# One ring of buffers for every loaded weight, float64 pieces converted in place, and other assumptions for loads in the list schedule

## The chip, the cores and the metric

The kernel runs on one core of one Trainium2 chip. The metric is the device time of one execution in microseconds, the median of several runs. The engines are TensorE (PE: products, and PEld: its weight loads), VectorE (DVE), ScalarE (ACT), GpSimd (POOL) and SyncE (SP, which here only issues transfers). Each works through its own list of instructions in order.

## The reference

Three layers follow one another on 1152 tokens of width 512: attention in a window of 64 positions, a layer of 8 experts where each token goes to one (with a capacity), and a dense layer:

```
h = x @ w_in                       # w_in  [512, 2048] float64
relu6 = np.clip(h + 3.0, 0.0, 6.0)
g = h * relu6 / 6.0
return (g @ w_out).astype(np.float32)   # w_out [2048, 512] float64
```

The expert layer computes `max(x @ w1[e], 0) @ w2[e]` with w1 [8, 512, 1024] and w2 [8, 1024, 512] in float32, times the gate's probability. [...]

## The kernel before, in words

**Products.** Every factor is kept as two float32r parts, high and low, and each product is three passes (high by high, low by high, high by low; `PASSES` and `mm`, L247-249). `split_ops` makes the two parts of a weight piece: ScalarE rounds it to the high part (L263), VectorE subtracts that for the low part (L268). Both go to a tile `wt`, of which there are eight halves.

**Units.** The work is cut into units of 256 columns of a hidden layer. 32 units (e0 to e31) belong to the experts, four to an expert, each with two halves of 512 KB that `weights_in` loads on the SP queue (L276 for w1, L279 for w2). Eight (d0 to d7) belong to the dense layer. A dense unit has four pieces of 512 KB of float64: pieces 0 and 1 from w_in for the up product, 2 and 3 from w_out for the down product. Eight expert units are tiny (64 tokens): TensorE multiplies their loaded float32 weights directly (L1468 up, L1493 down), so their buffers are held until the product has read them.

**Conversion.** A float64 piece arrives as 1024 words per partition, where low and high words alternate, so words of one kind lie 8 bytes apart. `conv64` turns it into 512 float32 values in six steps: ScalarE takes the absolute value of the high words (L207) and rounds them in place (L210); VectorE clamps (L214), shifts (L218), joins with the high words (L223) and adds the low words (L232, `t_add`).

**Buffers before.** Expert halves and the finished dense pieces share the ring `raw` of six buffers (4 KB per partition); float64 pieces have a ring of their own, `raw64`, of three. For d0 and d1 (`NSC = 2`) POOL's queue loads the pieces (L198, L201) during the expert stage, the converted pieces go from tiles `t64` to DRAM on the same queue (L235), and later come back as halves of `raw` (L1130). The pieces of d2 to d7 are loaded by SP and converted straight into halves of `raw`.

**The order of the work.** A list scheduler in Python writes the instructions. Products of TensorE and the steps that depend on them are written in a fixed order. Loads, conversions and splits are jobs with a due unit; `fill(limit)` (behind each product) emits the earliest due jobs whose estimated start fits before the limit, plus `SLACK` for engines or `SLACK_D` for loads, and `need` forces what a product is about to read. A load is assumed to have landed 2 us after its issue. A job's place in an engine's list is fixed once written; at run time an instruction waits for semaphores, and all behind it on that engine wait too.

**The dense layer.** It runs in four groups of tokens. The first takes tokens 0 to 639 through units d0 to d3, two steps of 128 columns for each: an up product (48 products of 320 tokens by three passes for two steps), then relu6 on ScalarE (L1554), its product with h on VectorE (`gf`, L1557), the split of that into `g` (L1560, L1563), and the down product of 15. The two parts of x come from L1384 on ScalarE and L1386 on VectorE.

Of the kernel before, what the change touches and what calls it, by code (L numbers as in the profile page):

```python
# [23 lines left out]
def tile_kernel(ctx, tc, q, k, v, w_gate, w1, w2, w_in, w_out, out, cap):  # L24
# [153 lines left out]
    NSC = 2  # L178
    cv = ctx.enter_context(tc.tile_pool(name="cv", bufs=2))
    wd_dram = [dram.tile([128, UW], F32, name=f"wd_dram{u}") for u in range(NSC)]  # L180
# [5 lines left out]
    def conv64(u, i, dst):  # L186

        box = {}  # L190

        queue = nc.gpsimd if u < NSC else nc.sync

        def load():
            box["raw"] = raw = cv.tile([128, 2 * HW], U32, name="raw64", bufs=NR64)
            if i < 2:
                src = w_in32[256 * i : 256 * i + 256, 2 * FU * u : 2 * FU * u + 2 * FU]
                queue.dma_start(raw.rearrange("p (c f) -> p c f", c=2), src.rearrange("(c p) f -> p c f", p=128))  # L198
            else:
                r0 = FU * u + 128 * (i - 2)  # L200
                queue.dma_start(raw, w_out32[r0 : r0 + 128, :])  # L201
            w = raw.rearrange("p (n t) -> p n t", t=2)
            box["lo"], box["hi"] = w[:, :, 0], w[:, :, 1]

        def c_abs():
            box["c"] = cv.tile([128, HW], U32, name="c64", bufs=NC64)
            nc.scalar.activation(box["c"].bitcast(F32), box["hi"].bitcast(F32), AF.Abs)  # L207
# [29 lines left out]
        return load, c_abs, c_round, c_clamp, c_shift, a_join, t_add, store  # L237

    NR64, NC64, NT64 = 3, 2, 2
# [83 lines left out]
    with ExitStack() as actx:  # L323
# [482 lines left out]
        def early_gather(e):  # L806
            box["xE"] = t = cv.tile([128, HW], U32, name="c64", bufs=NC64).bitcast(F32)
# [30 lines left out]
        def early_relu(u):  # L838
            def run(e):
                if "hfE" not in box:  # L840
                    box["hfE"] = cv.tile([128, HW], F32, name="t64", bufs=NT64)
                    box["hE"] = cv.tile([128, HW], F32, name="t64", bufs=NT64)
# [29 lines left out]
        def early_out(e):  # L872
            box["yE"] = t = cv.tile([128, HW], U32, name="c64", bufs=NC64).bitcast(F32)
# [87 lines left out]
        def first_gather(e):  # L961
            box["x0"] = t = cv.tile([128, HW], U32, name="c64", bufs=NC64).bitcast(F32)
# [59 lines left out]
    NRAW = 3  # L1022
# [8 lines left out]
    rawp = ctx.enter_context(tc.tile_pool(name="rawp", bufs=2 * NRAW))  # L1031
# [36 lines left out]
    SLACK, SLACK_D = 0.5, 4.0  # L1068
    BIAS = {"V": 0.6, "A": 0.1}
    AHEAD = (3.0, 1.5)  # L1070
    ZDUE = 3
# [25 lines left out]
    r_raw, r_wt, r_64, r_ct, r_t = Ring(2 * NRAW), Ring(2 * NWT), Ring(NR64), Ring(NC64), Ring(NT64)  # L1097
# [6 lines left out]
    wt_at, raw_at = {}, {}  # L1104
    for m in range(len(units)):
        for h in range(2):
            raw_at[m, h] = len(raw_at)
            if not whole(m):
                wt_at[m, h] = len(wt_at)
    raw_t, raw_ready, wt, half_ready, stored, pieces = {}, {}, {}, {}, {}, {}  # L1110
# [7 lines left out]
    def load_job(m, h):  # L1118
        kind, s, u = units[m]

        def gate():
            if kind == "d" and stored.get((u, h), 0) < 2:
                return None
            return r_raw.free(raw_at[m, h])

        def run(e, fin):
            take_raw(m, h)
            t = raw_t[m, h]
            if kind == "d":
                nc.gpsimd.dma_start(t, wd_dram[u][:, HALF * h : HALF * h + HALF])  # L1130
            else:
                if u == 0:
                    e_of[s] = expert(s)
                x = e_of[s]
                weights_in(t, x, u, h)
            raw_ready[m, 2 * h] = raw_ready[m, 2 * h + 1] = fin + 2.0
            if whole(m):
                half_ready[m, h] = fin + 2.0
# [4 lines left out]
    def conv_job(u, i, m=None):  # L1143
        h = i // 2
        ix = {}

        def dst():
            return None if m is None else raw_t[m, h][:, HW * (i % 2) : HW * (i % 2) + HW]

        load, c_abs, c_round, *mid, t_add, store = conv64(u, i, dst)  # L1150

        def gate_load():
            a = 0.0 if m is None or (m, h) in raw_t else r_raw.free(raw_at[m, h])
            b = r_64.free()
            return None if a is None or b is None else max(a - 2.0, b)

        def run_load(e, fin):
            if m is not None and (m, h) not in raw_t:
                take_raw(m, h)
            ix["raw"] = r_64.take()  # L1160
            load()
            return (fin if m is not None else spend("D", 1.46, fin)) + 2.0
# [13 lines left out]
        def run_add(e, fin):  # L1176
            if m is None:
                ix["t"] = r_t.take()
            t_add()
            r_64.rel[ix["raw"]] = r_ct.rel[ix["ct"]] = fin  # L1180
            if m is not None:
                raw_ready[m, i] = fin + 0.2
            return fin + 0.2

        def run_store(e, fin):
            store()
            r_t.rel[ix["t"]] = fin + 5.0
            stored[u, h] = stored.get((u, h), 0) + 1
            return fin

        now = lambda: 0.0
        ops = [({"D": 1.46} if m is not None else {"P": 1.1}, gate_load, run_load), ({"A": 0.6}, r_ct.free, run_abs)]
        ops.append(({"A": 0.57}, now, plain(c_round)))
        ops += [({"V": c}, now, plain(fn)) for c, fn in zip((0.34, 0.34, 0.61), mid)]
        ops.append(({"V": 0.61}, now if m is not None else r_t.free, run_add))
        return ops + ([({"P": 1.1}, now, run_store)] if m is None else [])
# [791 lines left out]
```

## Time and profile before

| | |
|---|---|
| median of 3 runs | 435.39 us (435.08 to 438.6) |
| profiled execution | 434.86 us, of which the span of the trace is 432.9 |
| PE busy | 406.1 us, 94% |
| DVE busy | 290.0 us, 67% |
| ACT busy | 241.4 us, 56% |
| DMA moved | 73.89 MB, 171 GB/s on average |
| granted clock of TensorE | 0.992 over the span |

Busy shares are means over stages that differ. The attention ends near 65 us, the expert stage runs to about 222, the first group of the dense layer from there to 277, and the other groups to the end. In the trace w_in and w_out of the dense layer are called `in_moe_w_in_dram` and `in_moe_w_out_dram`, the expert weights `in_moe_w_dram`, and both `raw` and `raw64` are called `raw`.

### The profile page before, as it was taken

How to read it: one execution, taken by the hardware profiler on the slowest of the kernel's cores; microseconds unless marked ns; L12 is line 12 of the kernel's file. 1: busy time of each engine (PE TensorE's matmuls, PEld its weight loads, DVE VectorE, ACT ScalarE, POOL GpSimd, SP SyncE). 2: the span in 40 equal slices, each digit the busy share in tenths (PEclk: the TensorE clock that was granted, in tenths of full speed). 3: DMA queues.
4: the chain of work that ended last, by engine and by line, in shares of the span. 5: the costliest groups of instructions: out<-in, count | busy, mean ns of one | idle time of the engine just before them, and what ended most of it. 6: DMA issues, size and time to landing. Idle time of an engine off the chain costs nothing.

```text
span 432.9 us, 8533 instructions
## 1 busy us (share of the span) xinstructions
PE 406.1 (94%) x3055; PEld 345.4 (80%) x3055; DVE 290.0 (67%) x800; ACT 241.4 (56%) x527; POOL 62.5 (14%) x128
## 2 busy tenths in 40 slices
PE   7999888798899999999999999999999999999991
PEld 4887664597778989987899898888888888899981
DVE  2888967687789999717579999989843222323430
ACT  4886773584569887526587766577543222322320
POOL 8633405025022001000200000000000000200210
PEclk9999999999999999999999999999999999999996
DMA  9997857989999999656924465543100000100101
GB/s 172 203 232 179 273 216 233 363 288 372 364 313 372 287 344 286 198 180 216 385 91 135 117 172 162 150 142 105 44 0 0 2 0 2 60 37 2 49 30 51
DMA packets 67762, 73.89 MB, mean 171 GB/s; under 512 B 31008, under 2 KB 49440, under 8 KB 67712
## 3 DMA queue, kind: packets, MB, share of 16 engines
q1 hardware_dynamic: 63760, 59.79, 46.6%
q0 software_dynamic: 3952, 13.47, 8.4%
q8 instruction: 26, 0.43, 0.4%
q14 instruction: 24, 0.20, 0.1%
HBM read 66.44 MB, written 6.82 MB: 169 GB/s over the span
## 4 chain that ended last, share of the span: by engine, by line
PE 65%; DVE 14%; DMA 10%; ACT 5%; issue 3%; POOL 0%; POOLq 0%; ACTq 0%; DVEq 0%; SPq 0%
PE banks L249 52%; DVE wt L268 4%; DMA raw<-in_moe_w_dram 4%; PE banks L506 2%; DMA c<-x_dram,eI 2%; PE banks L624 2%; DMA c<-x_dram,sidx 1%; PE banks L1493 1%; PE banks L1468 1%; PE banks L570 1%; PE banks L606 1%; DVE c L223 1%; DVE g L1563 1%; PE banks L663 1%; ACT wt L263 1%
## 5 line engine op out<-in xcount | busy, mean ns | idle before, releaser
L249 PE MATMUL banks<-x,wt 128*128 128x320 f32 (+3 forms) x576 | 107.4, 337 | 1.8 <-DVE wt L268 1.4
L249 PEld LDWEIGHTS banks<-x,wt 128*128 128x128 f32 x576 | 94.3, 188 | 12.2 <-DVE wt L268 2.2
L268 DVE TENSOR_TENSOR wt<-raw,wt 128x512 fp32r<-128x512 f32 x128 | 82.8, 684 | 14.9 <-ACT wt L263 14.3
L249 PE MATMUL banks<-wt,g 128*128 128x512 f32 x384 | 92.8, 390 | 0.0
L263 ACT CAST wt<-raw 128x512 fp32r<-128x512 f32 x128 | 74.6, 620 | 15.8 <-DMA raw<-in_moe_w_dram 9.4
L249 PEld LDWEIGHTS banks<-wt,g 128*128 128x128 f32 x384 | 71.6, 188 | 14.2
L1557 DVE SCALAR_TENSOR_TENSOR gf<-r,banks 128x320 f32<-128x320 f32 (+3 forms) x48 | 26.5, 552 | 54.5 <-ACT r L1554 54.3
L1554 ACT ACTIVATE r<-banks,c_three 128x320 f32<-128x320 f32 (+3 forms) x48 | 27.8, 579 | 58.3 <-PE banks L249 58.1
L249 PE MATMUL banks<-xT,wt 128*128 128x256 f32 (+2 forms) x288 | 39.0, 284 | 0.5 <-DVE wt L268 0.3
L249 PEld LDWEIGHTS banks<-xT,wt 128*128 128x128 f32 x288 | 35.1, 191 | 2.7 <-DVE wt L268 0.8
L249 PE MATMUL banks<-h,wt 128*128 128x256 f32 (+2 forms) x288 | 37.0, 279 | 0.0
L249 PEld LDWEIGHTS banks<-h,wt 128*128 128x128 f32 x288 | 34.6, 191 | 0.5 <-issue 0.5
L1563 DVE TENSOR_TENSOR g<-gf,g 128x320 fp32r<-128x320 f32 (+2 forms) x40 | 23.4, 584 | 12.3 <-ACT g L1560 11.6
L207 ACT ACTIVATE c<-raw 128x512 f32<-128x512 f32 x32 | 21.7, 677 | 17.1 <-DVE raw L232 6.3
L1560 ACT CAST g<-gf 128x320 fp32r<-128x320 f32 (+2 forms) x40 | 21.3, 533 | 16.3 <-DVE gf L1557 16.2
L1600 POOL DMA_INDIRECT out_dram<-raw,cidx x4 | 4.0, 992 | 163.8 <-ACT raw L1597 156.2
L249 PE MATMUL banks<-wt,xT 128*128 128x256 f32 x144 | 22.1, 294 | 3.0 <-DVE wt L268 2.2
L249 PEld LDWEIGHTS banks<-wt,xT 128*128 128x128 f32 x144 | 18.7, 190 | 5.7 <-DVE wt L268 3.6
L596 ACT ACTIVATE pe<-neg,nmx 128x128 f32<-128x128 f32 x72 | 22.3, 392 | 0.1
L583 DVE CUSTOM_DVE_ANT_0 neg<-banks,tmask 128x128 f32<-128x128 f32 x72 | 16.2, 285 | 9.1 <-PE banks L570 9.1
L223 DVE SCALAR_TENSOR_TENSOR c<-raw,c 128x512 uint32<-128x512 uint32 x32 | 22.0, 686 | 0.4
L210 ACT ACTIVATE raw<-raw 128x512 uint32<-128x512 uint32 x32 | 21.6, 674 | 0.0
(287 smaller groups left out, 556.0 us busy)
## 6 DMA issues: line engine op xcount, KB each, us to landing
raw<-in_moe_w_dram SPq DMA_DIRECT2D x64, 512.0 KB, 6.0
raw<-in_moe_w_in_dram SPq DMA_DIRECT2D x12, 512.0 KB, 3.8
raw<-in_moe_w_out_dram SPq DMA_DIRECT2D x12, 512.0 KB, 3.7
early<-in_moe_w_dram SPq DMA_DIRECT2D x8, 512.0 KB, 7.3
x_dram<-xt SPq DMA_DIRECT2D x9, 256.0 KB, 2.9
q_sb<-in_q_dram SPq DMA_DIRECT2D x8, 256.0 KB, 4.8
k_sb<-in_k_dram SPq DMA_DIRECT2D x8, 256.0 KB, 4.8
v_sb<-in_v_dram SPq DMA_DIRECT2D x8, 256.0 KB, 4.7
```

The lines of the kernel that those rows point to most:

```text
L207: nc.scalar.activation(box["c"].bitcast(F32), box["hi"].bitcast(F32), AF.Abs)
L210: nc.scalar.activation(box["lo"], box["lo"], AF.Copy, scale=2.0 ** -29)
L223: nc.vector.scalar_tensor_tensor(out=box["c"], in0=box["hi"], scalar=0xC0000000, in1=box["c"], op0=ALU.bitwise_and, op1=ALU.bitwise_or,)
L249: nc.tensor.matmul(out, l, r, start=(start and n == 0), stop=(stop and n == len(pairs) - 1))
L263: nc.scalar.copy(hi, r)
L268: V.tensor_tensor(out=lo, in0=r, in1=hi.bitcast(F32), op=ALU.subtract)
L583: V.tensor_tensor_reduce(out=neg[:, hp, :], in0=box["sp", g][:, hp, :], in1=tmask[:, first, :], scale=-1.0, scalar=3.0e38, op0=ALU.add, op ...
L596: nc.scalar.activation(pe[:, hp, :], neg[:, hp, :], AF.Exp, bias=nmx[:, hp : hp + 1], scale=-1.0)
L1554: nc.scalar.activation(r, ph, AF.Relu, bias=c_three)
L1557: V.scalar_tensor_tensor(out=gf, in0=r, scalar=6.0, in1=ph, op0=ALU.min, op1=ALU.mult)
L1560: nc.scalar.copy(hi, gf)
L1563: V.tensor_tensor(out=lo, in0=gf, in1=hi.bitcast(F32), op=ALU.subtract)
```

## The change

There is one ring of eight `raw` buffers for all loads: expert halves and float64 pieces alike, all on the SP queue. It takes as much memory as the two rings, `t64` and the extra tiles did. `t_add` writes its 512 results over the low words of the piece itself, 8 bytes apart, and the splits read them there. d0's four pieces are converted when units 5, 9, 14 and 20 are due (`FIRST_AT`), into four contiguous tiles `first_w`, which stay until the dense layer begins. d1 is converted like d2 to d7, 1.5 units before its use. The stores to DRAM and the reloads are gone. The scheduler takes a load to have landed 3.5 us after its issue, and may write a load 40 us ahead of the limit rather than 4. The order of TensorE's products is the same. The buffers of the early expert (`hfE`, `hE`) are now `first_w[0]` and `first_w[1]`.

```diff
-    def conv64(u, i, dst):
+    def conv64(u, i, dst=None):
         box = {}
-        queue = nc.gpsimd if u < NSC else nc.sync
         def load():
-            box["raw"] = raw = cv.tile([128, 2 * HW], U32, name="raw64", bufs=NR64)
+            box["raw"] = raw = rawp.tile([128, 2 * HW], F32, name="raw").bitcast(U32)
             if i < 2:
                 ...
         def t_add():
-            d = dst()
-            if d is None:
-                box["t"] = d = cv.tile([128, HW], F32, name="t64", bufs=NT64)
-            nc.vector.tensor_tensor(out=d.bitcast(U32), in0=box["c"], in1=box["lo"], op=ALU.add)
-
-        def store():
-            nc.gpsimd.dma_start(wd_dram[u][:, HW * i : HW * i + HW], box["t"])
+            out = box["lo"] if dst is None else dst.bitcast(U32)
+            nc.vector.tensor_tensor(out=out, in0=box["c"], in1=box["lo"], op=ALU.add)
+        return box, (load, c_abs, c_round, c_clamp, c_shift, a_join, t_add)
-    NR64, NC64, NT64 = 3, 2, 2
+    NC64 = 2
+    first_w = [cv.tile([128, HW], F32, name=f"first_w{i}", bufs=1) for i in range(4)]
...
-    NRAW = 3
+    NRAW = 8
+    FIRST_AT = (5, 9, 14, 20)
-    rawp = ctx.enter_context(tc.tile_pool(name="rawp", bufs=2 * NRAW))
+    rawp = ctx.enter_context(tc.tile_pool(name="rawp", bufs=NRAW))
-    SLACK, SLACK_D = 0.5, 4.0
+    SLACK, SLACK_D = 0.5, 40.0
...
+    dense0 = unit_of["d", 0, 0]
     for m in range(len(units)):
+        if m != dense0:
+            for n in range(2 if units[m][0] == "e" else NPC):
+                raw_at[m, n] = len(raw_at)
+            for i in range(NPC):
+                if FIRST_AT[i] == m:
+                    raw_at[dense0, i] = len(raw_at)
...
         def run(e, fin):
             take_raw(m, h)
-            t = raw_t[m, h]
-            if kind == "d":
-                nc.gpsimd.dma_start(t, wd_dram[u][:, HALF * h : HALF * h + HALF])
-            else:
-                ...
-            raw_ready[m, 2 * h] = raw_ready[m, 2 * h + 1] = fin + 2.0
+            ...
+            raw_ready[m, 2 * h] = raw_ready[m, 2 * h + 1] = fin + 3.5
...
         def run_low(e, fin):
             ...
+            if units[m][0] == "d" and m != dense0:
+                r_raw.rel[raw_at[m, i]] = fin
...
-            if kind == "d" and u >= NSC:
-                add_job(m - AHEAD[1] + 0.1 * i, m, conv_job(u, i, m))
+            if m == dense0:
+                add_job(FIRST_AT[i] + 1, FIRST_AT[i], conv_job(m, i))
             elif kind == "d":
-                add_job(m + ZDUE + 0.1 * i, m, conv_job(u, i))
-        if kind == "e" or u < NSC:
+                add_job(m - AHEAD[1] + 0.1 * i, m, conv_job(m, i))
+        if kind == "e":
```

**POOL's list in the expert stage, before.** L801 gathers token rows; L198 and L201 load float64 pieces, L235 stores converted ones.

```order
L801 DMA xg<-x_dram,sidx 64x512
L198 DMA raw_1552<-in_moe_w_in_dram 128x2x512
L198 DMA raw_1554<-in_moe_w_in_dram 128x2x512
L201 DMA raw_1568<-in_moe_w_out_dram 128x1024
L235 DMA wd_dram_101<-t_1666 128x512
L201 DMA raw_1708<-in_moe_w_out_dram 128x1024
L801 DMA xg<-x_dram,sidx 128x512
L235 DMA wd_dram_101<-t_1781 128x512
L198 DMA raw_1826<-in_moe_w_in_dram 128x2x512
L801 DMA xg<-x_dram,sidx 128x512
L235 DMA wd_dram_101<-t_1807 128x512
```

The same place after the change, where gathers are L791:

```order
L1852 CAST eofI_1448<-eofF 128x8
L791 DMA xg<-x_dram,sidx 128x512 x2
L791 DMA xg<-x_dram,sidx 64x512
L791 DMA xg<-x_dram,sidx 128x512 x2
L791 DMA xg<-x_dram,sidx 96x512
L791 DMA xg<-x_dram,sidx 128x512 x2
L791 DMA xg<-x_dram,sidx 80x512
```

Only the gathers are left; the eight loads went to SP's list, the stores and the reloads have no successor.

**VectorE's list at the start of the dense layer, before.** It begins with the two low parts of x. L214, L218, L223 and L232 here convert d2; `gf` and `g` belong to the first up products; wt_3483 is the up half of d1 (third up product).

```order
L1386 TENSOR_TENSOR x2_1616<-banks_82,x2_1616 128x2x208
L214 TENSOR_SCALAR c64_3533<-c64_3533 128x512
L218 TENSOR_SCALAR c64_3533<-c64_3533 128x512
L1557 SCALAR_TENSOR_TENSOR gf_3537<-r6_3536,banks_82 128x320
L223 SCALAR_TENSOR_TENSOR c64_3533<-raw64_3410,c64_3533 128x512
L214 TENSOR_SCALAR c64_3542<-c64_3542 128x512
L1563 TENSOR_TENSOR g_3520<-gf_3537,g_3520 128x320
L1557 SCALAR_TENSOR_TENSOR gf_3562<-r6_3561,banks_82 128x320
L218 TENSOR_SCALAR c64_3542<-c64_3542 128x512
L232 ISA raw_3409<-raw64_3410,c64_3533 128x1024
L1563 TENSOR_TENSOR g_3520<-gf_3562,g_3520 128x320
```

The same place after, with L1363 for L1386, L208, L212, L217 and L224 for the conversion, L258 for the split, L1534 for `gf`. wt_3358 is the up half of d0; raw_3299 and raw_3301 are the last two pieces of d1.

```order
L1363 TENSOR_TENSOR x2_1614<-banks_82,x2_1614 128x2x208
L258 TENSOR_TENSOR wt_3358<-first_w1_102,wt_3358 128x512
L212 TENSOR_SCALAR c64_3413<-c64_3413 128x512
L217 SCALAR_TENSOR_TENSOR c64_3413<-raw_3299,c64_3413 128x512
L224 ISA raw_3299<-raw_3299,c64_3413 128x512x2
L208 TENSOR_SCALAR c64_3472<-c64_3472 128x512
L212 TENSOR_SCALAR c64_3472<-c64_3472 128x512
L217 SCALAR_TENSOR_TENSOR c64_3472<-raw_3301,c64_3472 128x512
L1534 SCALAR_TENSOR_TENSOR gf_3502<-r6_3501,banks_82 128x320
L208 TENSOR_SCALAR c64_3499<-c64_3499 128x512
L224 ISA raw_3301<-raw_3301,c64_3472 128x512x2
```

Two instructions of a conversion stood between x and the first `gf`; now a split of d0 and six of d1's conversion do. Before, all four splits of d0 stood ahead of x; now three of them follow it, the two of its down half between the `gf` further on, and the splits of d1's up half (wt_3509) come after those.

## Rows read from the trace of the kernel before

**Rows 1.** The page's part 1, busy time and share of the span.

```profile
PE 406.1 (94%) x3055; PEld 345.4 (80%) x3055; DVE 290.0 (67%) x800; ACT 241.4 (56%) x527; POOL 62.5 (14%) x128
```

**Rows 2.** Table by stretches: length, busy us of each engine, clock, DMA share, GB/s.

```profile
85.00:130.00 45.00, 41.45 (x335) 35.79 (x334) 35.99 (x91) 28.35 (x62) 11.61 (x16) 1.00 0.99 335
...
180.00:222.20 42.20, 41.56 (x355) 35.61 (x353) 21.69 (x48) 21.43 (x51) 2.19 (x4) 1.00 0.69 235
222.20:277.30 55.10, 53.33 (x299) 48.01 (x299) 51.60 (x106) 38.34 (x75) 0.00 (x0) 1.00 0.46 133
```

**Rows 3.** Waits of TensorE, 85 to 280 us: total us, times, longest.

```profile
PE banks L249 <- DVE wt L268: 3.8, 5, 1.2
PE banks L1468 <- DMA raw<-in_moe_w_dram: 1.1, 1, 1.1
PE banks L249 <- ACT wt L263: 0.6, 1, 0.6
```

**Rows 4.** DMA from 70 to 130 us: sum, software queue, issues with us to landing.

```profile
DMA packets 11812, 20.16 MB, mean 336 GB/s; under 512 B 728, under 2 KB 6892, under 8 KB 11806
...
q0 software_dynamic: 2144, 7.41, 34.2%
...
raw<-in_moe_w_dram SPq DMA_DIRECT2D x25, 512.0 KB, 8.2
raw<-in_moe_w_in_dram POOLq DMA_DIRECT2D x4, 512.0 KB, 8.7
raw<-in_moe_w_out_dram POOLq DMA_DIRECT2D x4, 512.0 KB, 7.3
wd_dram<-t POOLq DMA_DIRECT2D x7, 256.0 KB, 6.2
```

**Rows 5.** Chain of waits that ended last: start us, length, what.

```profile
100.60 12.88 DMA raw<-in_moe_w_dram
```

**Rows 6.** Waits of the SP queue, 60 to 130 us.

```profile
SPq L276 <- PE banks L1468: 11.3, 3, 9.7
```

**Rows 7.** TensorE's timeline: start us, length, shape, [wait before, releaser].

```profile
110.76 2.19 PE L249 MATMUL banks<-xT,wt 128*128 128x256 f32 x12
...
118.20 1.60 PE L249 MATMUL banks<-xT,wt 128*128 128x256 f32 x12
...
199.07 1.94 PE L249 MATMUL banks<-wt,xT 128*128 128x256 f32 x12
...
223.14 7.01 PE L249 MATMUL banks<-x,wt 128*128 128x320 f32 x46 [0.36 <-ACT x L1384]
...
233.42 3.68 PE L249 MATMUL banks<-x,wt 128*128 128x320 f32 x24
...
248.90 3.51 PE L249 MATMUL banks<-x,wt 128*128 128x320 f32 x20 [0.86 <-DVE wt L268]
...
264.15 2.90 PE L249 MATMUL banks<-x,wt 128*128 128x320 f32 x18 [0.50 <-DVE wt L268]
```

**Rows 8.** VectorE's timeline at the dense layer's start.

```profile
223.69 0.43 DVE L214 TENSOR_SCALAR c<-c 128x512 f32<-128x512 f32 x1
224.15 0.43 DVE L218 TENSOR_SCALAR c<-c 128x512 uint32<-128x512 uint32 x1
225.47 0.49 DVE L1557 SCALAR_TENSOR_TENSOR gf<-r,banks 128x320 f32<-128x320 f32 x1 [0.90 <-ACT r L1554]
...
232.70 1.28 DVE L268 TENSOR_TENSOR wt<-raw,wt 128x512 fp32r<-128x512 f32 x2
233.90 0.68 DVE L223 SCALAR_TENSOR_TENSOR c<-raw,c 128x512 uint32<-128x512 uint32 x1
234.62 0.69 DVE L232 CUSTOM_DVE_ANT_0 raw<-raw,c 128x1024 uint16<-128x1024 uint16 x1
```

**Rows 9.** The page's part 5, costliest groups: busy us, mean ns of one.

```profile
L223 DVE SCALAR_TENSOR_TENSOR c<-raw,c 128x512 uint32<-128x512 uint32 x32 | 22.0, 686 | 0.4
L210 ACT ACTIVATE raw<-raw 128x512 uint32<-128x512 uint32 x32 | 21.6, 674 | 0.0
```

More of the change, by code (lines that the diff above doesn't have):

```diff
@@ L177, in tile_kernel @@
     HW = UW // 4
-    NSC = 2
     cv = ctx.enter_context(tc.tile_pool(name="cv", bufs=2))
-    wd_dram = [dram.tile([128, UW], F32, name=f"wd_dram{u}") for u in range(NSC)]
     w_in32 = w_in.bitcast(U32)
@@ L840, in run @@
                 if "hfE" not in box:
-                    box["hfE"] = cv.tile([128, HW], F32, name="t64", bufs=NT64)
-                    box["hE"] = cv.tile([128, HW], F32, name="t64", bufs=NT64)
+                    box["hfE"] = first_w[0]
+                    box["hE"] = first_w[1]
                 if e == "A":
@@ L1118, in load_job @@
     def load_job(m, h):
-        kind, s, u = units[m]
+        _, s, u = units[m]
         def gate():
-            if kind == "d" and stored.get((u, h), 0) < 2:
-                return None
             return r_raw.free(raw_at[m, h])
@@ L1127, in run, with conv_job @@
             take_raw(m, h)
-            t = raw_t[m, h]
-            if kind == "d":
-                nc.gpsimd.dma_start(t, wd_dram[u][:, HALF * h : HALF * h + HALF])
-            else:
[L1132 to L1135, printed above, removed]
-            raw_ready[m, 2 * h] = raw_ready[m, 2 * h + 1] = fin + 2.0
+            if u == 0:
+                e_of[s] = expert(s)
+            weights_in(raw_t[m, h], e_of[s], u, h)
+            raw_ready[m, 2 * h] = raw_ready[m, 2 * h + 1] = fin + 3.5
             if whole(m):
-                half_ready[m, h] = fin + 2.0
+                half_ready[m, h] = fin + 3.5
             return fin
         return [({"D": 1.46}, gate, run)]
-    def conv_job(u, i, m=None):
-        h = i // 2
+    def conv_job(m, i):
+        u = units[m][2]
         ix = {}
[L1147 to L1155, printed above, removed]
+        first = m == dense0
+        b, (load, c_abs, c_round, *mid, t_add) = conv64(u, i, first_w[i] if first else None)
         def run_load(e, fin):
-            if m is not None and (m, h) not in raw_t:
-                take_raw(m, h)
-            ix["raw"] = r_64.take()
+            r_raw.take()
             load()
-            return (fin if m is not None else spend("D", 1.46, fin)) + 2.0
+            raw_t[m, i] = first_w[i] if first else b["lo"].bitcast(F32)
+            return fin + 3.5
         def run_abs(e, fin):
@@ L1176, in run_add @@
         def run_add(e, fin):
[L1177 to L1178 removed]
             t_add()
[L1180 to L1182 removed]
+            r_ct.rel[ix["ct"]] = fin
+            if first:
+                r_raw.rel[raw_at[m, i]] = fin
+            raw_ready[m, i] = fin + 0.2
             return fin + 0.2
[L1185 to L1189, printed above, removed]
         now = lambda: 0.0
[L1192 removed]
+        ops = [({"D": 1.46}, lambda: r_raw.free(raw_at[m, i]), run_load), ({"A": 0.6}, r_ct.free, run_abs)]
         ops.append(({"A": 0.57}, now, plain(c_round)))
         ops += [({"V": c}, now, plain(fn)) for c, fn in zip((0.34, 0.34, 0.61), mid)]
[L1195 to L1196 removed]
+        ops.append(({"V": 0.61}, now, run_add))
+        return ops
     def split_job(m, i):
@@ L1211, in run_high @@
             n = HALF // 2
-            r = raw_t[m, h][:, n * (i % 2) : n * (i % 2) + n]
+            r = raw_t[m, h][:, n * (i % 2) : n * (i % 2) + n] if units[m][0] == "e" else raw_t[m, i]
             high, box["low"] = split_ops(wt[m, h], r, i % 2)
@@ L1675, in dense_again @@
                 for i in range(NPC):
-                    r = wk.tile([128, HW], F32, name="xg", bufs=3)
-                    if u < NSC:
-                        nc.sync.dma_start(r, wd_dram[u][:, HW * i : HW * i + HW])
-                    else:
-                        load, *mid, t_add, _ = conv64(u, i, lambda: r)
-                        for fn in (load, *mid, t_add):
-                            fn()
+                    b, ops = conv64(u, i)
+                    for fn in ops:
+                        fn()
+                    r = b["lo"].bitcast(F32)
                     high, low = split_ops(halves[i // 2], r, i % 2)
@@ L1872, in tile_kernel @@
     est["D"] = max(est["D"], done["rk"] + 1.7)
-    for ring, t in ((r_64, est["P"]), (r_ct, done["g0"] + 4.0), (r_t, done["g0"] + 4.0)):
+    for ring, t in ((r_ct, done["g0"] + 4.0),):
         ring.rel = [t] * ring.n
```

24 lines of the change are left out of this document (12 added, 12 removed).

## The prediction, made before the changed kernel ran

> **What bounds the kernel now.** I read the page's busy times first: TensorE is busy for 406.1 of 432.9 us [rows 1], so at most 27 us of waits can be won, and adding work to another engine costs only where TensorE then waits for it. The table by stretches came next [rows 2]. The stretch from 85 to 130 us has the DMA engines at a share of 0.99 with TensorE 3.55 us short of full; from 180 to 222 VectorE is half idle (21.69 of 42.20 us); from 222 to 277, the first group of the dense layer, VectorE is busy for 51.60 of 55.10 us and TensorE lacks 1.77. So two stretches have little room, one in DMA and one in VectorE, and between them lies one with room in both. Third, the waits of TensorE from 85 to 280 us [rows 3]: 3.8 us for the split weights `wt` of VectorE (five waits), 1.1 for a load, 0.6 for `wt` of ScalarE. Two of the five VectorE waits, 0.86 and 0.50, stand in the dense group [rows 7], which leaves 3.8 - 1.36 = 2.44 in the expert stage.
>
> Who makes them late? The DMA view of 70 to 130 us [rows 4] has 20.16 MB at 336 GB/s; 7.41 MB of it are on the software queue, where the conversion of d0 and d1 lives: eight loads of 512 KB (4 + 4) and seven stores of 256 KB. A load of expert weights takes 8.2 us to land there. In the chain of waits one load holds 12.88 us from 100.60 [rows 5], with the late splits right behind it. And the SP queue itself stood for 9.7 us on the first product of a tiny expert (L1468), whose buffer the next load in line needed [rows 6]: with six buffers, no load could pass it.
>
> **The change part by part.**
>
> *Expert stage.* Removed: eight loads on POOL, eight stores, four reloads (POOL's rows in the order go from stores and loads between the gathers to gathers alone). Added: eight loads on SP, four of them spread at units 5, 9, 14 and 20, of which two fall before unit 10. Of the traffic between 70 and 130 us, 8 x 0.5 + 7 x 0.25 = 5.8 MB go and about 1 MB comes back, 4.8 MB or 14 us at 336 GB/s [rows 4]. The ring grows from six to eight, and by the order of the loads and the count of buffers 15 loads rather than 10 can be issued ahead of the first tiny product. VectorE loses d1's conversions here (four pieces of four instructions), which stand in the same stretch. All three point at the same waits: 2.44 + 1.1 + 0.6 = 4.1 us, plus two products that ran stretched without a recorded wait, 2.19 and 1.94 where the same shape takes 1.60 [rows 7], 0.6 + 0.35. That is 5.0 us in all. Bounds: 0 if the waits only change their cause; the 5.0 plus nothing, since the shorter waits here are for h, which the change doesn't touch. I take -5.0: the load that the chain names now has 14 us of traffic less ahead of it, over its 12.88 us.
>
> *The dense start.* The conversion of d1 moves to just before its use, beside d2's. d0 is already converted, but three of its four splits, and d1's last two conversions, now stand on VectorE behind the second low part of x (the order's rows on VectorE). VectorE runs in order, so I price the list. Two independent splits start 0.60 us apart (1.28 for two, of 0.68 each); 16 instructions from 225.47 to 232.70 take 7.23 us, four of them of the wide kind, so the others cost (7.23 - 2.4) / 12 = 0.40; a wide instruction that needs the result of the one before starts after 0.72 (233.90 to 234.62) rather than 0.60, a narrow one after 0.46 (223.69 to 224.15) [rows 8].
> (a) The first product's second low part of `wt` starts at 223.69 at the earliest, when that slot held an L214 before [rows 8], and is ready 0.69 later, at 224.4. TensorE resumed at 223.14 and comes to it four products (0.15 each, 7.01 for 46) on [rows 7], 223.7: +0.7.
> (b) From 223.69 to the second low part of the third up product there are 27 instructions, 12 wide: 12 x 0.60 + 15 x 0.40 + 0.3 for dependent neighbours = 13.5, so ready at 237.2, and its first low part at 236.6. Before, up product three began at 233.42 [rows 7]; it asks for the first low part four products later, 234.0, and with (a) 234.7. The wait is 1.9, and 0.3 more for the second: 2.2.
> (c) To the fifth up product's second low part 30 more, 13 wide: 7.8 + 6.8 + 0.5 = 15.1, ready at 252.3 and 251.7. TensorE asks at 248.04 (248.90 less its wait of 0.86 [rows 7]) plus 2.9, 250.9: 0.8 + 0.3 = 1.1.
> Behind it the list has fewer instructions per step than TensorE has time for, and the 0.50 of the seventh product goes. Together 0.7 + 2.2 + 1.1 = 4.0 after against 0.86 + 0.50 = 1.36 before: **+2.6**. Bounds: +0.5 if d1's pieces get their VectorE time during 180 to 222 us, and TensorE only finds (a); +4 if the loads of d1 land late too.
>
> *In place and spaced.* `t_add` now writes words 8 bytes apart, and the splits read them so. Before had no such write by VectorE. The nearest rows: L223 reads words so spaced in 686 ns, and ScalarE's L210 reads and writes them so in place in 674 [rows 9], against 0.68 for a split of contiguous words [rows 8]. I take 0; the upper bound, a doubling, is a rival below.
>
> *The rest.* SLACK_D and the later landing only reorder SP's queue, where nothing else is queued behind the loads. The four reloads lay where DMA had a share of 0.69 [rows 2]: 0. The early expert's `hfE` and `hE` in `first_w` are read before d0's first conversion: 0.
>
> **Sum.** -5.0 + 2.6 = -2.4 on the profiled execution's 434.86 us: 432.5. The median of the runs shown (435.39) stands 0.53 above that execution, so the forecast for the median is **433.0**.
>
> **Rivals.**
> 1. *The dense start costs nothing.* Units d0 and d1 have their pieces on hand early, VectorE is half idle from 180 to 222 [rows 2], and the list catches up before the first product. Against it: the order is fixed, and the pieces stand behind x. Only -5.0, at best 0.5 off: 435.39 - 5.0 = 430.4. Chance 0.27.
> 2. *The dense start eats all.* d1's loads share the ring with the last tiny units, so that they issue only when those are used; conversions then begin late and the +4 of the bound, with about 1 more behind it, cancels the gain: 435.4. Chance 0.15.
> 3. *The ring doesn't do what it says.* A load still waits in line behind a tiny unit's buffer, as in [rows 6]: the waits stay, and the dense start's 2.6 is added: 438.0. Chance 0.06.
> 4. *Slower: spaced words at half speed on VectorE.* Twelve `t_add` of d1 to d3 lie in the dense group, where VectorE had 3.5 us free [rows 2]. Doubled from 0.68, they add 12 x 0.68 = 8.2 us, all of it on the list TensorE waits for: 433.0 + 8.2 = 441.2, and more if the splits double as well. It decides from about 1.2 us for one. Against it L223 and L210 [rows 9]. Chance 0.07.
> 5. *No overlap on VectorE.* If each instruction of the list cost its whole length, 0.69 for a wide one and 0.46 for a narrow one (the ends from [rows 8]), (b) would take 12 x 0.69 + 15 x 0.46 = 15.2 in place of 13.5, and (c) 16.8 in place of 15.1: +3.4, so 436.4. Two splits of 0.68 in 1.28 us [rows 8] speak against it. Chance 0.02. The Trainium skill ("VectorE: DVE Perf Modes", section "The DRAIN you can't avoid") states this rule, that the next operation doesn't start until the pipeline is empty; by that rule the trace would show 1.36 for the two splits, so it disagrees here, although its page adds that an operation that isn't held starts earlier.
>
> **How the numbers follow.** The forecast case has 0.43, with a range of its own of 431 to 435. The 8-in-10 range takes in rival 1 down to 428.5 (the waits gone and a little of the dense group's own too) and rivals 2 and 5 up to 437.5; it leaves out 4, most of 3 and the tails. A measurement of this kernel tells 1%, about 4.4 us, from no change. Faster by more (under 431.0) is most of rival 1 and the low tail of the forecast: 0.28. Slower by more (over 439.7) is rival 4 with the tails of 2 and 3: 0.12. Within 1%: 0.60.
>
> **What would show it.** Right: between 105 and 125 us the waits for `wt` and for a load are gone, the software queue carries only gathers, the dense layer starts near 217 rather than 222, and TensorE waits some 2 us for VectorE's `wt` in the third up product and 1 in the fifth. `t_add` keeps its 0.69. Wrong: a load's wait of several us at a tiny unit (rival 3), waits in the dense group under 1 us (1) or over 5 (2), `t_add` above 1.2 us (4), or a new wait between 130 and 215 where the list now places d0's pieces.

## The result, and the profile after

The changed kernel takes 429.14 us (median of four runs, 428.49 to 429.65) against 435.24 for the kernel before; the ratio is 0.9865 (0.9826 to 0.9904). The profiled execution took 428.49 us, of which the span of the trace is 426.8. The forecast was 433.0: faster, as it came, but 2.4 us faster where it was 6.1. The time lies inside the range of 428.5 to 437.5, 0.6 above its lower end, and in the case "under 431.0", which had a chance of 0.28.

To see where the 6 us lie, I cut each trace at four marks that every version has: the first gather product of 64 tokens (L1317, after the change L1294), the first product of the dense layer, the first product of its second group of tokens, and the issue of the last scatter (POOL). The lengths in us come from the timelines; two of the four columns are from second profiles, of the unedited kernels, taken with the experiments (runs before_again and after_again).

| stage | before | before again | after | after again |
|---|---|---|---|---|
| start to L1317 | 87.35 | 89.18 | 85.88 | 86.09 |
| of there, to L1304 (L1281) of the next team | 40.80 | 39.05 | 36.89 | 36.91 |
| L1317 to the dense layer | 134.86 | 134.58 | 129.65 | 129.65 |
| first dense group | 55.05 | 54.83 | 56.79 | 57.72 |
| to the issue of the last scatter | 147.60 | 147.59 | 147.72 | 147.59 |
| from there to the end | 8.04 | 8.12 | 6.76 | 6.75 |

(The second row is a part of the third.) Between the first profiles: -1.5 at the start, -5.2 in the expert stage, +1.7 in the first dense group, +0.1, -1.3 at the very end: -6.1. The expert stage of one kernel is the same within 0.3 us in its two profiles, though the stretch in the second row is not (40.80 and 39.05 before). The start differs more: over all 14 profiles of this study it ended between 85.46 and 89.18.

The page's first part, and the table by stretches (length, busy us of each engine, clock, DMA share, GB/s), which answers [rows 1, 2]:

```profile
PE 403.8 (95%) x3055; PEld 344.1 (81%) x3055; DVE 290.3 (68%) x801; ACT 242.3 (57%) x526; POOL 50.6 (12%) x108
```

```profile
85.00:130.00 45.00, 44.43 (x366) 38.70 (x365) 32.82 (x84) 27.54 (x63) 3.79 (x3) 1.00 0.91 300
...
180.00:216.00 36.00, 36.00 (x312) 31.15 (x310) 22.18 (x46) 22.63 (x52) 0.00 (x0) 1.00 0.74 246
216.00:271.00 55.00, 52.02 (x291) 46.53 (x291) 53.67 (x112) 38.73 (x76) 0.00 (x0) 1.00 0.36 115
```

From 85 to 130 us TensorE lacks 0.57 us where it lacked 3.55, and the DMA engines' share is 0.91 rather than 0.99; VectorE in the dense group is fuller still, 53.67 of 55.00. DMA from 70 to 130 us, beside [rows 4]:

```profile
DMA packets 12710, 18.62 MB, mean 310 GB/s; under 512 B 635, under 2 KB 7821, under 8 KB 12704
...
q0 software_dynamic: 592, 1.90, 9.0%
...
raw<-in_moe_w_dram SPq DMA_DIRECT2D x29, 512.0 KB, 6.8
```

The software queue fell from 7.41 MB to 1.90, and a load lands in 6.8 us rather than 8.2, while 29 of them fit where 25 did. TensorE's waits that are left (start, length, shape, wait before):

```profile
143.82 0.93 PE L239 MATMUL banks<-xT,wt 128*128 128x224 f32 x6 [1.45 <-DVE wt L258]
...
217.72 6.42 PE L239 MATMUL banks<-x,wt 128*128 128x320 f32 x42 [0.38 <-DVE wt L258]
223.98 3.59 PE L239 MATMUL banks<-wt,g 128*128 128x512 f32 x15
227.41 0.74 PE L239 MATMUL banks<-x,wt 128*128 128x320 f32 x4
229.81 3.50 PE L239 MATMUL banks<-x,wt 128*128 128x320 f32 x20 [1.67 <-DVE wt L258]
233.15 3.59 PE L239 MATMUL banks<-wt,g 128*128 128x512 f32 x15
...
243.52 0.74 PE L239 MATMUL banks<-x,wt 128*128 128x320 f32 x4
244.71 3.50 PE L239 MATMUL banks<-x,wt 128*128 128x320 f32 x20 [0.45 <-DVE wt L258]
248.05 3.59 PE L239 MATMUL banks<-wt,g 128*128 128x512 f32 x15
```

The waits of [rows 3] in the expert stage are gone but for 0.47 us near 106 to 110; a new one of 1.45 stands at 143.82. In the dense group the waits stand at the first, third and fifth up product, as the list said. On VectorE there, beside [rows 8]:

```profile
216.99 0.68 DVE L258 TENSOR_TENSOR wt<-first_w,wt 128x512 fp32r<-128x512 f32 x1
217.58 0.42 DVE L212 TENSOR_SCALAR c<-c 128x512 uint32<-128x512 uint32 x1
...
220.90 0.48 DVE L1534 SCALAR_TENSOR_TENSOR gf<-r,banks 128x320 f32<-128x320 f32 x1
...
229.07 1.29 DVE L258 TENSOR_TENSOR wt<-raw,wt 128x512 fp32r<-128x512 f32 x2
```

The split of d0 takes the slot that an L214 had, and the two splits for the third up product begin at 229.07: the first is ready at 229.76, and TensorE resumes at 229.81.

### The profile page after: what moved, and what is told of

It reads as the page before. It is cut to its first block, busy times and chain, and to the rows that moved or that the text cites. A ratio compares the mean times of both kernels' runs of the same rounds, so it can differ in the third digit from the quotient of the medians.

```text
span 426.8 us, 8494 instructions
## 1 busy us (share of the span) xinstructions
PE 403.8 (95%) x3055; PEld 344.1 (81%) x3055; DVE 290.3 (68%) x801; ACT 242.3 (57%) x526; POOL 50.6 (12%) x108
## 4 chain that ended last, share of the span: by engine, by line
PE 70%; DVE 16%; DMA 4%; ACT 3%; issue 3%; SPq 1%; POOL 0%; POOLq 0%; ACTq 0%; DVEq 0%
PE banks L239 58%; DVE wt L258 5%; PE banks L1445 2%; PE banks L496 2%; PE banks L614 2%; PE banks L1470 2%; DMA c<-x_dram,sidx 1%; DVE neg L573 1%; PE banks L596 1%; DMA v_sb<-in_v_dram 1%; DVE raw L224 1%; DVE c L217 1%; PE banks L560 1%; SPq L464 1%; ACT wt L253 1%
## 5 line engine op out<-in xcount | busy, mean ns | idle before, releaser
L258 DVE TENSOR_TENSOR wt<-raw,wt 128x512 fp32r<-128x512 f32 x124 | 80.1, 687 | 14.6 <-ACT wt L253 14.4
L253 ACT CAST wt<-raw 128x512 fp32r<-128x512 f32 x124 | 73.0, 631 | 7.8 <-PE banks L239 5.9
L1534 DVE SCALAR_TENSOR_TENSOR gf<-r,banks 128x320 f32<-128x320 f32 (+3 forms) x48 | 26.5, 552 | 53.5 <-ACT r L1531 53.4
L201 ACT ACTIVATE c<-raw 128x512 f32<-128x512 f32 x32 | 21.5, 673 | 11.0 <-DVE raw L224 8.9
L217 DVE SCALAR_TENSOR_TENSOR c<-raw,c 128x512 uint32<-128x512 uint32 x32 | 22.0, 689 | 0.7
L573 DVE CUSTOM_DVE_ANT_0 neg<-banks,tmask 128x128 f32<-128x128 f32 x72 | 16.2, 285 | 8.8 <-PE banks L560 8.8
L791 POOL DMA_INDIRECT xg<-x_dram,sidx x10 | 12.7, 1271 | 79.6 <-PE banks L1281 70.1
L239 PE MATMUL banks<-wt,xT 128*128 128x256 f32 x144 | 20.6, 290 | 0.3 <-DVE wt L258 0.2
```

What stands on the lines that cost most here:

```text
L217: nc.vector.scalar_tensor_tensor(out=box["c"], in0=box["hi"], scalar=0xC0000000, in1=box["c"], op0=ALU.bitwise_and, op1=ALU.bitwise_or,)
L239: nc.tensor.matmul(out, l, r, start=(start and n == 0), stop=(stop and n == len(pairs) - 1))
L253: nc.scalar.copy(hi, r)
L258: V.tensor_tensor(out=lo, in0=r, in1=hi.bitcast(F32), op=ALU.subtract)
L573: V.tensor_tensor_reduce(out=neg[:, hp, :], in0=box["sp", g][:, hp, :], in1=tmask[:, first, :], scale=-1.0, scalar=3.0e38, op0=ALU.add, op ...
L1534: V.scalar_tensor_tensor(out=gf, in0=r, scalar=6.0, in1=ph, op0=ALU.min, op1=ALU.mult)
```

## The experiments

Lengths are of the same stages as above; "expert" is from L1317 to the dense layer, "dense" the first dense group. Each ratio is to the kernel before as timed beside that run (its medians lie between 433.7 and 436.4), so ratios can be compared where medians of different rows can't.

| run | median, us | ratio to before | L1317 to L1304 | expert | dense | end |
|---|---|---|---|---|---|---|
| late_conv | 437.3 | 1.0032 (0.9997 to 1.0067) | 36.90 | 137.81 | 55.04 | 8.04 |
| ring6 | 449.25 | 1.0301 (1.0247 to 1.0356) | 41.17 | 145.80 | 60.82 | 6.82 |
| traffic | 432.32 | 0.9918 (0.9893 to 0.9944) | 36.89 | 131.52 | 56.79 | 7.61 |
| late_traffic | 445.03 | 1.0225 (1.0152 to 1.0297) | 44.09 | 144.79 | 55.03 | 9.25 |
| ahead06 | 425.66 | 0.9765 (0.9718 to 0.9812) | 36.89 | 129.65 | 53.52 | 6.80 |
| sched_old | 430.03 | 0.9879 (0.9818 to 0.9941) | 35.69 | 127.38 | 58.96 | 6.78 |
| first_late | 427.24 | 0.9799 (0.9737 to 0.9861) | 36.89 | 131.14 | 52.89 | 7.04 |
| tiny | 431.14 | 0.9894 (0.9836 to 0.9951) | 36.91 | 129.65 | 56.77 | 8.62 |
| tiny_sp | 428.77 | 0.9867 (0.9797 to 0.9937) | 36.90 | 129.63 | 57.74 | 6.58 |
| both_06 | 423.87 | 0.9758 (0.9705 to 0.9812) | 35.69 | 127.33 | 53.52 | 6.65 |
| after_again | 429.13 | 0.9876 (0.9813 to 0.9938) | 36.91 | 129.65 | 57.72 | 6.75 |
| before_again | 435.15 | 1.0001 (0.9953 to 1.0049) | 39.05 | 134.58 | 54.83 | 8.12 |

**What held the loads back: late_conv, ring6, traffic, late_traffic.** My theory was that the traffic and work of converting d0 and d1 made the expert weights late; the rival was the ring of six alone.

The first edit is to the kernel before:

```diff
-    for ring, t in ((r_64, est["P"]), (r_ct, done["g0"] + 4.0), (r_t, done["g0"] + 4.0)):
+    for ring, t in ((r_64, est["P"] + 50.0), (r_ct, done["g0"] + 4.0), (r_t, done["g0"] + 4.0)):
```

> The kernel before, but its float64 buffers count as free 50 us later, so that the conversion of d0 and d1 (POOL loads, stores, VectorE and ScalarE work) starts after about 125 us; the ring stays at six. Theory T (the traffic and the work of these conversions held the expert weights back): the stretch from the product L1481 at 106.25 to L1304 at 128.15, 21.9 us before and 17.9 in the changed kernel, falls to 18 to 19, and the median by 3 to 5 us, to 430 to 432. Theory R (six buffers, blocked by tiny units, held the loads back): the stretch stays at 21 to 22 and the median within 1 us of before.

The stretch fell to 36.90, what the changed kernel has, with a ring of six; 0.2 us of TensorE's waits are left between 85 and 130 us. The gap between the two marks of before and of this run:

```profile
87.35 0.46 PE L1317 MATMUL banks<-ident,xg 64*128 64x64 f32 x4
...
128.15 0.60 PE L1304 MATMUL banks<-ident,xg 128*128 128x128 f32 x4
```

```profile
88.41 0.46 PE L1317 MATMUL banks<-ident,xg 64*128 64x64 f32 x4
...
125.31 0.60 PE L1304 MATMUL banks<-ident,xg 128*128 128x128 f32 x4
```

So taking the conversions away is enough for this stretch, and in the SP queue no wait at L1468 is longer than 1.9 us, where [rows 6] have 9.7: six buffers alone did not make that wait. The median did not follow, against my number: the conversions came back between 150 and 222 us, where TensorE then waited 1.19 and 1.58 us for h and 0.98 for `wt` of ScalarE, and the expert stage grew by 3 us, of which some 1.6 are products at a lower clock behind the last of these waits (last section).

```diff
-    NRAW = 8
+    NRAW = 6
```

> The changed kernel with a ring of six buffers in place of eight. Theory R: the same stretch grows from 17.9 back to 20 to 22 us. Theory T: it stays within 0.5 us of 17.9. In both, the dense start gets worse, since by VectorE's list the second low part of the third up product stands 17.5 us after the low part of x rather than 13.7: its wait grows from 1.7 to about 5, and the median by about 4.

The stretch grew to 41.17, with no load or store of POOL in it. The SP queue's waits from 60 to 130 us show why:

```profile
SPq L266 <- DVE first_w L224: 7.9, 1, 7.9
```

The load next in line needed the buffer of a float64 piece of d0 that was not yet converted. When one ring holds both kinds, six are too few; the dense group got worse by 4.0, as expected from the list. The median grew by 20 us, though, not by about 4: the expert stage is 16.2 longer, of which 4.3 in this stretch. Behind it TensorE goes on waiting for splits (1.19 us at 129.53, 1.91 at 154.81), and from 132 to 134 us the granted clock was 0.50.

```diff
     def gather_ahead(s, i):
         ...
+        count.append(0)
+        if len(count) == 3:
+            for j in range(10):
+                nc.gpsimd.dma_start(spare[j % 2], w_in32[0:128, 0:1024])
```

> The changed kernel with ten transfers of 512 KB from DRAM to DRAM added on POOL after the seventh gather (about 87 us), two at a time; they compute nothing. Theory T: the stretch between the same two products grows from 17.9 by 2 to 4 us, with waits for the split weights or loads between 95 and 125 us. Theory R: by less than 0.5 us, since the eight buffers let the loads go early enough.

The first theory failed here. From 85 to 125 us (sum, then loads with their us to landing) the DMA engines were fuller than in the kernel before (346 GB/s there), and a load took longer (8.2 us there):

```profile
DMA packets 8723, 15.42 MB, mean 385 GB/s; under 512 B 491, under 2 KB 4648, under 8 KB 8718
...
raw<-in_moe_w_dram SPq DMA_DIRECT2D x18, 512.0 KB, 11.0
```

Yet the stretch stayed at 36.89. With eight buffers a load may take 11.0 us rather than 6.0, and TensorE doesn't notice it in this stretch; what the transfers cost (1.9 us) came right behind it, by 132 us.

> The run late_conv (six buffers, conversions of d0 and d1 after 125 us) with the ten DRAM to DRAM transfers of the run traffic added on POOL from about 88 us; they compute nothing. There the stretch from L1481 at 106 to L1304 at 128 took 17.9 us. If six buffers can't hide loads that land later, the traffic alone brings it back to 20 to 22 us (8 buffers with the same traffic kept 17.9). If it was the conversions' own work on VectorE and ScalarE, it stays at 18 to 18.5. The median stays between 437 and 441, since late conversions still cost what they cost there.

The same transfers (the edit of traffic on top of that of late_conv), with six buffers: 44.09, more than I had given it, and a median of 445 rather than at most 441. ScalarE waited 9.20 us for one load, and TensorE for ScalarE:

```profile
129.13 0.62 ACT L263 CAST wt<-raw 128x512 fp32r<-128x512 f32 x1 [9.20 <-DMA raw<-in_moe_w_dram]
```

```profile
122.05 1.09 PE L1475 MATMUL banks<-raw,xT 128*64 128x128 f32 x16 [0.88 <-DMA raw<-in_moe_w_dram]
...
130.09 0.69 PE L1437 MATMUL banks<-ident,hf 128*128 128x128 f32 x2 [5.33 <-ACT hf L1431]
```

The delayed conversions' first three loads (from 121.39) fell into the end of this stretch, so the 7.2 us are not those of the ten transfers alone. All of them came behind 121 us: the product at 120.09 stands 33.25 us behind the first mark, as in late_conv (33.26), though the DMA engines were full up to there (share 0.99, second column from the end):

```profile
87.00:123.00 36.00, 34.68 (x287) 29.84 (x286) 18.52 (x54) 15.50 (x37) 8.25 (x14) 1.00 0.99 338
```

Up to the same product before took 37.16 us. So at six buffers transfers alone cost nothing there, and before's 3.9 us have more causes than loads that land late. Its trace shows three:

```profile
105.83 0.69 DVE L232 CUSTOM_DVE_ANT_0 t<-raw,c 128x1024 uint16<-128x1024 uint16 x1 [2.87 <-DMA wd_dram<-t]
...
107.50 2.49 DVE L268 TENSOR_TENSOR wt<-raw,wt 128x512 fp32r<-128x512 f32 x4
...
122.27 2.48 DVE L268 TENSOR_TENSOR wt<-raw,wt 128x512 fp32r<-128x512 f32 x4
```

```profile
108.24 1.58 PE L249 MATMUL banks<-wt,xT 128*128 128x256 f32 x8 [1.25 <-DVE wt L268]
...
115.69 1.09 PE L1468 MATMUL banks<-raw,xT 128*64 128x128 f32 x16 [1.08 <-DMA raw<-in_moe_w_dram]
...
123.00 1.58 PE L249 MATMUL banks<-wt,xT 128*128 128x256 f32 x8 [0.92 <-DVE wt L268]
```

At 105.83 VectorE stood for 2.87 us until an earlier converted piece had been stored from its `t64` tile to DRAM, with the splits of an expert unit behind it in its list; TensorE went on after the first of them. The second wait is for a load. Ahead of the splits at 122.27 VectorE's list has eight steps of conversions, from 117.52 on. Compared product by product with late_conv, before lost 0.95, 1.15 and 1.7 us there. Its second profile has the same wait for a store (2.69 us) and one for a load (0.54), and lost, against after_again, 2.1 us in this stretch and 1.7 right behind it.

What the runs show, then: without the conversions of d0 and d1 six buffers are enough here; with eight buffers and neither d1's conversion nor the stores, ten added transfers change nothing here. Eight buffers with before's conversions were not run, so whether the deeper ring by itself would have removed before's waits is not shown. The three shares are read from the trace, not from an experiment on each.

**What sets the dense start: ahead06, first_late.** The edit to the changed kernel:

```diff
-    AHEAD = (3.0, 1.5)
+    AHEAD = (3.0, 0.6)
```

> The changed kernel with d1 to d7 converted 0.6 units before their use rather than 1.5. If the order of VectorE's list makes the waits at the dense start: all four splits of d0 now stand ahead of x, and the low parts of the third up product come 8.1 and 9.7 us after the low part of x rather than 13.0 and 13.7, so the waits of 0.38, 1.67 and 0.45 us go, the dense group (first product of it to first of the next, 56.8 us) falls to about 54, and the median from 429.1 to 426 to 427. If instead the landing of d1's loads or ScalarE's part sets it, later conversions make the group longer, 57 to 60 us, and the median 430 or more.

The dense group fell to 53.52 us and the median to 425.66. No wait for a split of VectorE is recorded in it; TensorE's timeline there:

```profile
217.94 7.01 PE L239 MATMUL banks<-x,wt 128*128 128x320 f32 x46 [0.40 <-ACT x L1361]
...
228.22 3.96 PE L239 MATMUL banks<-x,wt 128*128 128x320 f32 x24
...
242.38 4.04 PE L239 MATMUL banks<-x,wt 128*128 128x320 f32 x24
```

The third and fifth up products are only stretched, 3.96 and 4.04 for 3.68. So the order of VectorE's list made the waits, not the landing of d1's loads: loading and converting later made it faster, since d0's splits then stand ahead of x.

On top of it, `FIRST_AT = (5, 9, 22, 26)`:

> The run ahead06 with the last two pieces of d0 converted at units 22 and 26 rather than 14 and 20. If the wait of 1.45 us for the split weights near 145 us comes from the conversion that stands before it in VectorE's list (2.4 us of work where VectorE is busy for 19.0 of 20 us), it goes, and the median falls from 425.7 by 1 to 1.5, to 424 to 425. If VectorE's list is late there anyway, the wait stays above 1 us and the median within 0.5.

Half of this held. The wait of 1.45 near 145 us went, but the median came out at 427.24 rather than 424 to 425: the conversions now stood before other splits, near 190 us:

```profile
190.67 1.70 PE L239 MATMUL banks<-wt,xT 128*128 128x256 f32 x10 [0.64 <-ACT wt L253]
...
196.40 0.98 PE L239 MATMUL banks<-wt,xT 128*128 128x256 f32 x6 [1.43 <-DVE wt L258]
```

The expert stage is 1.5 longer, the dense group 0.6 shorter. VectorE's idle time from 180 us on, which I had counted as free, isn't free at every place in its list.

**The scheduler's assumptions: sched_old, both_06.**

```diff
-    SLACK, SLACK_D = 0.5, 40.0
+    SLACK, SLACK_D = 0.5, 4.0
...
-            raw_ready[m, 2 * h] = raw_ready[m, 2 * h + 1] = fin + 3.5
+            raw_ready[m, 2 * h] = raw_ready[m, 2 * h + 1] = fin + 2.0
```

(and so at the two other places that have 3.5).

> The changed kernel with the old assumptions of the scheduler: a load has landed 2.0 us after its issue, and is written at most 4 us ahead. If these assumptions matter, splits are written where their loads have not landed, VectorE waits there, and TensorE's waits in the expert stage grow by 2 us or more (431 to 434). If the ring and the removed traffic do it all, the median stays within 1 us of 429; by the list, the first product of the dense group waits about 0.7 more.

The median is within 1 us of the changed kernel's, but not because nothing happens: the expert stage is 2.3 us shorter, where I had longer waits in view, and the dense group 2.2 longer. In these two stages the new assumptions of the change gain nothing in sum; they move a loss from one to the other. Which of the two numbers does it was not tried.

> The changed kernel with d1 to d7 converted 0.6 units before their use (the edit of ahead06) and the old assumptions of the scheduler for loads (the edit of sched_old). The expert stage of sched_old had no wait of TensorE between 85 and 162 us and ended 7.6 us earlier than before's, that of ahead06 5.2; ahead06 had no wait for the split weights in the dense group. If the two edits act in separate stages, the median is 2 us under ahead06's 425.7, at 423 to 424.5. If the old assumptions cost again at the dense start what they win before it, it stays at 425 to 427.

With ahead06's order at the dense start the loss there has no place to go, and both gains stay: expert 127.33, dense 53.52, median 423.87 against 429.13 for the changed kernel (after_again), timed beside it. It beats both kernels. Its waits from 85 to 290 us are:

```profile
PE banks L1281 <- DVE xg L1273: 0.5, 1, 0.5
PE banks L239 <- ACT x L1361: 0.4, 1, 0.4
```

**The end of the program: tiny, tiny_sp.** The first adds this at the seventh call of `gather_ahead`, the second twenty such transfers by `nc.sync` where the last dense group begins (each to a tile of its own, where the first has two in turn):

```diff
+            for j in range(20):
+                nc.gpsimd.dma_start(spare[j % 2], w_in32[0:1, 0:512])
```

> The changed kernel with twenty transfers of 2 KB added on POOL after the last gather (about 162 us), when POOL has nothing else to do; they compute nothing. From the issue of the last scatter to the end the kernel before takes 8.0 us and the changed one 6.8, for the same instructions; the run traffic, with ten more transfers on POOL, took 7.6. If transfers on POOL's queue set it, it grows to about 8 us here, and the median by 1.2 to 430.3. If not, it stays at 6.8 and the median within 0.5.

> The changed kernel with twenty transfers of 2 KB added on SP's queue where the last group of the dense layer begins; they compute nothing. In the run tiny the same transfers on POOL's queue made the time from the issue of the last scatter to the end 8.6 us in place of 6.8. If that belongs to POOL's queue, it stays at 6.8 to 7.0 here; if to the number of transfers, it grows to 8 or more.

The end grew to 8.62 us with the transfers on POOL and stayed, at 6.58, with them on SP. The last scatter of before, after, tiny and tiny_sp, whose spans are 432.9, 426.8, 429.1 and 427.0:

```profile
424.86 0.97 POOL L1600 DMA_INDIRECT out_dram<-part,cidx  x1 [3.11 <-DVE part L1591]
```

```profile
420.04 0.97 POOL L1577 DMA_INDIRECT out_dram<-part,cidx  x1 [3.25 <-DVE part L1568]
```

```profile
420.48 0.97 POOL L1584 DMA_INDIRECT out_dram<-part,cidx  x1 [3.21 <-DVE part L1575]
```

```profile
420.42 0.97 POOL L1581 DMA_INDIRECT out_dram<-part,cidx  x1 [3.11 <-DVE part L1572]
```

Over all profiles the end follows the number of transfers on POOL's queue over the changed kernel's: none 6.58 to 7.04, ten 7.61, twenty (before, before_again, late_conv, tiny) 8.04 to 8.62, thirty (late_traffic) 9.25.

**The two kernels once more: after_again, before_again.**

> The changed kernel once more, unedited, beside the two others of this call: 0.985 to 0.988 of before, 429 us. In its profile the stretch from L1294 near 86 us to L1281 near 123 us takes 36.9 us again, and the dense group 56.8. Its start, up to 87 us, was 1.5 us ahead of before's in the first profile; if that belongs to the change, it is so again, and if it varies from run to run, it lies anywhere between -1.8 and +1.1 as in the other runs.

> The kernel before, unedited, for a second profile. In the ten other runs the product L1317/L1294 near 87 us came 1.9 us earlier to 1.1 us later than in the first profile of before. If the start of the changed kernel gains about 1.4 us by the change, this profile has it within 0.3 us of 87.35; if it varies from run to run, it can be as far off as the others. The stretch from there to L1304 takes 40.8 us again, the dense group 55.05, and the end behind the last scatter 8.0.

The expert stage is the same to 0.01 us in the two profiles of after, and to 0.28 in those of before. The stretch to L1304 missed its number in before_again: 39.05 rather than 40.8, so late_conv's 36.90 is 2.1 to 3.9 us under before's. The start is not before's own: its second profile reached L1317 at 89.18. Before's four versions with POOL's conversions lie at 86.84 to 89.18, the ten with the change at 85.46 to 87.42; whether the change gives a part of that stays open. One difference goes with the scheduler's numbers: in all six profiles with the old ones (before's four, sched_old, both_06) TensorE waits 1.35 to 3.10 us at a gather product near 80 us (L1304, after the change L1281), for nothing that the profile shows, and in none of the eight with the new ones. In the dense group after_again missed its number: 57.72, which the last section takes up.

## Why the prediction was right, and where it was not

- **The expert stage, -5.0: right in size, in part by luck,** -5.2 and -4.9 in the two pairs. TensorE's products have the same order in both kernels, so they can be compared one by one: in the first pair the stage won 6.9 us and lost 1.7, of which 1.5 at the new wait at 143.82, which I had only named as a way to be wrong. The two errors of the sum, waits that were worth more than their records and a new wait, nearly cancel. The 0.6 for the product of 2.19 us in [rows 7] did not come: it takes 2.19 us again in the changed kernel, from 108.35 on. The reason was half right. I took the size from the traffic ahead of the loads, with VectorE's conversions beside it; of the 3.9 us to 128 us the trace of before has 1.15 at a load, 1.7 behind conversions in VectorE's list, and 0.95 behind a wait of VectorE for a store, which the prediction doesn't have.
- **The dense start, +2.6: mis-sized, +1.74.** The terms of after were right one by one: (a) 8.45 us from the first product to the first down product against 7.78, +0.67 for a forecast of 0.7; (b) 5.74 against 3.51 from the third up product to its down product, +2.23 for 2.2; (c) 4.53 against 3.51, 1.02 for 1.1. The list itself took 13.37 us from 216.99 to the end of the second split (229.07 + 1.29), for a forecast of 13.5. The term that failed is what stood there before, "0.86 + 0.50 = 1.36". Those are recorded waits. Before's fifth and seventh up products show the whole delay:

```profile
247.30 0.74 PE L249 MATMUL banks<-x,wt 128*128 128x320 f32 x4
...
252.25 3.59 PE L249 MATMUL banks<-wt,g 128*128 128x512 f32 x15
...
262.61 1.04 PE L249 MATMUL banks<-x,wt 128*128 128x320 f32 x6
...
266.89 3.59 PE L249 MATMUL banks<-wt,g 128*128 128x512 f32 x15
```

  From start to start, 4.95 and 4.28 us where an undisturbed one takes 3.51: 1.44 + 0.77 = 2.21, and 0.67 + 2.23 + 1.02 - 2.21 = +1.71, against a measured step of 1.74. A wait's record leaves out the time in which the products before and behind it run slower.
- **In place and spaced, 0: right.** `t_add` takes 688 ns on words 8 bytes apart, against 687 for before's form, and a split 687 on average against 684, so rival 4 is out:

```profile
L224 DVE CUSTOM_DVE_ANT_0 raw<-raw,c 128x1024 uint16<-128x1024 uint16 x28 | 19.3, 688 | 0.9
```

- **The rest, 0: wrong by 1.3.** I costed the twenty transfers that leave POOL's queue only where they ran. At the program's end they were worth 1.28 us.
- **The scheduler's numbers, 0: right in sum over the expert stage and the dense group, wrong as an account,** +2.3 in one and -2.2 in the other (sched_old against after).
- **The start,** -1.5 in the first pair, was in no term. The wait near 80 us that goes with the scheduler's old numbers could be a part of it; that stays open.
- **The rivals.** The median came out beyond rival 1, yet not by its mechanism: the dense start did cost. Rival 5, no overlap on VectorE, would have made the list 15.2 us; it took 13.37. By the rule in the Trainium skill ("VectorE: DVE Perf Modes", "The DRAIN you can't avoid") that the next operation waits until the pipeline is empty, it would have been the longer one; the trace agrees with the exception in the same section, that an operation that isn't held starts earlier.

## What to carry to other kernels

Price a moved piece of work by the in-order list that it lands in: the order of VectorE's list told the three delays of the dense start to 0.1 us, and the idle share of the stage told none. Measure a stall from product to product, not by the recorded wait. Before you put a late split on its load, read what the engine that makes it waited for earlier in its list: here one such wait was for a store.

## What the hardware showed beyond that

Transfers on POOL's queue, though all were issued more than 200 us before the end, made the end behind the last scatter longer, by 0.06 to 0.09 us for each on average (twenty: 1.28 to 1.86), and twenty on SP's queue did not. Why they do is not shown.

TensorE's clock fell in two of the five profiles that share the changed kernel's list at the dense start (after_again and tiny_sp; not in after, tiny and traffic). In after_again, where TensorE had done nothing from 228.3 to 230.0 (clock in the third column from the end):

```profile
229.00:230.00 1.00, 0.00 (x0) 0.00 (x0) 1.00 (x3) 1.00 (x2) 0.00 (x0) 1.00 0.00 0
...
231.00:232.00 1.00, 1.00 (x7) 1.00 (x6) 0.93 (x4) 0.81 (x2) 0.00 (x0) 0.69 0.81 123
232.00:233.00 1.00, 1.00 (x5) 1.00 (x5) 0.86 (x2) 1.00 (x3) 0.00 (x0) 0.50 0.98 360
233.00:234.00 1.00, 1.00 (x6) 1.00 (x5) 1.00 (x3) 1.00 (x3) 0.00 (x0) 0.50 1.06 410
234.00:235.00 1.00, 1.00 (x6) 1.00 (x5) 0.97 (x3) 0.93 (x2) 0.00 (x0) 0.61 0.41 156
```

Behind the wait of 1.67 us the granted clock went to 0.50, the lower of its two levels (1.2 of 2.4 GHz), for some 3.5 us, and twenty products took 5.04 us rather than 3.50. That made the dense group 57.72 rather than 56.79 us. The same wait in the profile of after left the clock at 1.00, so a wait of this length costs its own time and sometimes 0.9 us more. The drop can come behind a shorter wait too. In late_conv TensorE did nothing for 1.0 us (a recorded wait of 0.98), and three microseconds later the clock was at 0.50:

```profile
206.00:207.00 1.00, 0.02 (x1) 0.02 (x1) 0.97 (x4) 0.96 (x3) 0.62 (x1) 1.00 1.08 379
...
210.00:211.00 1.00, 1.00 (x3) 0.74 (x3) 1.00 (x4) 0.00 (x0) 0.00 (x0) 0.50 0.84 237
```
